# Reordering the start of a fused attention and token-mixing block on one core: loads, column sums, warm-up matmuls, early splits and the sums of phi(k)

## The chip, the cores and the metric

The kernel runs on one core of a Trainium2 chip. Its time is the device time of one execution in microseconds (us); the figure before the change is the median of three runs, and one more execution was taken with the hardware profiler. The engines are called as the profile calls them: PE is TensorE (PEld its weight loads), DVE is VectorE, ACT is ScalarE, POOL is GpSimd, SP is SyncE, which here only issues DMAs.

## The reference

`x` has S = 2048 tokens of D = 448 values. Two blocks follow each other, each with a modulated layer norm and a gated residual:

```python
mod = (silu(c) @ w_mod).reshape(1, 6, 1, 448)          # sa, ca, ga, sb, cb, gb
h = layernorm(x) * (1 + ca) + sa
x = x + ga * A(h)                                      # linear attention
h = layernorm(x) * (1 + cb) + sb
x = x + gb * B(h)                                      # token-mixing MLP

def A(x):                                              # 16 heads of 28
    q, k, v = split_heads(x @ wqkv)
    phi = lambda t: where(t > 0, t + 1, exp(t)) + 1e-6
    kv = einsum("hsd,hse->hde", phi(k), v); z = phi(k).sum(over s)
    return ((phi(q) @ kv) / (phi(q) . z + 1e-6)) @ wo

def B(x):                                              # F = 1792
    u = gelu(layernorm(x)^T @ w1 + b1)
    return (u @ w2 + b2)^T
```

Everything is fp32 in and out. The kernel splits an fp32 operand into a high and a low part (`hh` and `hl` for the token tiles, `wh` and `wl` for the weights, `pkh` and `pkl` for phi(k)) and sums the products of the parts on PE.

## The kernel before, in words

Tokens are cut into 16 tiles of 128 (`t`). The program is written out engine by engine in the order of the source (a manual schedule): each engine works through its own instructions in that order, and semaphores make it wait for the others' results. Buffers come from a pool of 74 slots that are used in turn, so a tile that is allocated waits until the last reader of the slot's former content is done. [...] DMAs are issued from SP's queue in the order of the source; those that add into their target (`accum_op`) are issued by POOL.

The stages follow each other: phase A computes q, k and phi(k) for all tiles and sums phi(k)^T x; then the small products with `wo`; then x is updated, normalised again and transposed; then the two big products with `w1` and `w2`. The change touches only the first part of phase A, roughly the first 90 us:

- `load_x(t)` fetches the tile x(t) for its statistics and `load_xt(t)` its transpose for the products; `load_first(j, ch)` fetches chunk `ch` of a transposed part of `w_mod` (`wt`), for j = 0 the shift and for j = 1 the scale.
- `spread` and `keep_warm(n)`: n matmuls of ones into a spare bank that keep PE busy until the first weights are there.
- `col_sum(j, ch)` multiplies a chunk with the spread silu(c) and sums it into one column of `col`. `row_part(1, ch)` adds the raw weights times a column of the shift to `accb`, one chunk after the other; `row_bias(1)` (L277) brings `accb` to PE, and `row_out(1)` makes the last rows of `wrow` of it, on ACT and then on DVE (L282).
- `projects(...)` and `close(t, 1)`: kp, the k part of tile t. It is accumulated from the parts without any layer norm and closed by one matmul with `wrow` and the rows of mean and root (L426).
- Those rows come from `a_stats_act` for tiles 0 and 1 (sums on ACT, two small steps and then the root as a power on POOL) and from `a_stats_dve` for the later pairs (statistics on DVE, `ve`, and the power on POOL, L339). `a_rows` writes them to `rowst` (L382, L385), `a_transpose` turns them on PE (`rw`, L391), and `a_copy` puts them into the last rows of `hl`.
- `a_split_high(t)` (ACT, L398) and `a_split_low(t)` (DVE, or POOL for tiles 0 and 2; L402) make `hh` and `hl`.
- `a_exp`, `a_pk` (DVE, L441) and `a_pk_parts` make phi(k), its high part and its low part. For tiles 3 to 12 the low part is finished by an adding DMA on POOL (L504); for tiles 2 to 12 a second adding DMA adds phi(k) into `pksum` (L508), which is read when the phase ends.
- `a_outer(t)` adds phi(k)^T x of a tile to `cacc`. The loop over t = 4 to 15 works four tiles behind on it (`KV_LAG`), and at t = 5, 7, 9 and 11 takes the statistics of the tiles t + 3 and t + 4.

Of the kernel before, what the change touches and what calls it, by code (L numbers as in the profile page):

```python
# [11 lines left out]
ALU = mybir.AluOpType  # L12
AX = mybir.AxisListType

P = 128
# [6 lines left out]
EPS = 1e-5  # L22
# [29 lines left out]
def block_kernel(ctx: ExitStack, tc: tile.TileContext, x, xt, wqkv, wo, w1, b1, w2, b2, c, wmod, wfirst, out):  # L52
# [69 lines left out]
    def load_x(t):  # L122
        X[t] = slot(f"x{t}")
        nc.sync.dma_start(X[t], xf[t * P:(t + 1) * P, :])
# [3 lines left out]
    def load_xt(t):  # L128
        XT[t] = slot(f"xt{t}", 512)
        nc.sync.dma_start(XT[t], xt[t])  # L130
# [8 lines left out]
    def load_first(j, ch, eng=nc.sync):  # L139
        wt[j, ch] = slot(f"wt{j}_{ch}", D + 1)  # L140
        eng.dma_start(wt[j, ch][:, :D], wfirst[j, ch])
        nc.gpsimd.memset(wt[j, ch][:, D:], 1.0 if j else 0.0)
# [12 lines left out]
    for ch in range(1, 4):  # L155
        load_first(1, ch)
        load_qkv(1, chs=(ch,))
        if ch == 1:
            load_xt(1)
    load_xt(2)  # L160
    for ch in range(4):
        load_first(0, ch)
    load_x(0)
    load_x(1)
    load_xt(3)
    load_xt(4)
    load_x(2)
# [14 lines left out]
    def keep_warm(n):  # L182
        for i in range(n):
            nc.tensor.matmul(warm[:, :P], ones, ones, start=True, stop=True)
# [30 lines left out]
    def col_sum(j, ch):  # L215
        if j not in col:
            col[j] = cst.tile([P, 4], F32, name=f"col{j}")
        p = slice(0, 64 if j == 0 and ch == 3 else P)
        w = wt.pop((j, ch))[p]
        nc.vector.scalar_tensor_tensor(w, w, 1.0, scr[p, :D + 1], op0=ALU.mult, op1=ALU.mult,  # L220
                                       accum_out=col[j][p, ch:ch + 1])
# [40 lines left out]
    def row_part(j, ch):  # L262
        if ch == 0:
            accb[j] = slot(f"accb{j}")
            nc.vector.tensor_scalar_mul(accb[j], raw_w[j, 0], col[0][:, 0:1])
        else:
            nc.vector.scalar_tensor_tensor(accb[j], raw_w[j, ch], col[0][:, ch:ch + 1], accb[j],
                                           op0=ALU.mult, op1=ALU.add)

    def row_sum(j):  # L270
        rowb[j] = bank(f"rowb{j}")
        ws = [Whi[j, ch] for ch in range(4)] + [Wlo[j, ch] for ch in range(3)]
        for i, w in enumerate(ws):
            nc.tensor.matmul(rowb[j][:ROWS, :D], sel_s, w, start=(i == 0), stop=False)
# [66 lines left out]
    def a_stats_act(ts):  # L341
        n = len(ts)
        g, ve = a_group(ts)
        sm = small.tile([P, n, 3], F32, name=f"as{ts[0]}", tag=f"as{n}")

        def one(i):
            t, s3 = ts[i], sm[:, i, :]
            nc.scalar.activation(junk, X[t], AF.Identity, accum_out=s3[:, 0:1])
            nc.scalar.activation(s3[:, 1:2], s3[:, 0:1], AF.Copy, scale=-1.0 / D)
            b_square(X[t], s3[:, 1:2], s3[:, 2:3], f"s{t}")  # L350

        def end():
            nc.gpsimd.tensor_scalar_mul(g[:, :, 0:1], sm[:, :, 0:1], 1.0 / D)
            nc.gpsimd.tensor_scalar(ve, sm[:, :, 2:3].to_broadcast([P, n, 2]), 1.0 / D, EPS,
                                    op0=ALU.mult, op1=ALU.add)
            a_pow(g, ve)
            groups[ts[0]] = g
        return one, end
# [37 lines left out]
    def a_split_high(t):  # L396
        heads[t] = (slot(f"hh{t}", 512, F32R), slot(f"hl{t}", 512, F32R))
        nc.scalar.activation(heads[t][0], XT[t], AF.Copy)  # L398

    def a_split_low(t):  # L400
        eng = nc.gpsimd if t in POOL_LOW else nc.vector
        eng.tensor_sub(heads[t][1], XT[t], heads[t][0].bitcast(F32))  # L402
        XT[t] = None

    def a_split(t):
        a_split_high(t)
        a_split_low(t)
# [88 lines left out]
    def a_pk_parts(t):  # L496
        pk = pkf.pop(t)
        hi, lo = moving(slot, f"pkh{t}"), moving(slot, f"pkl{t}")
        nc.scalar.activation(hi, pk, AF.Copy, bias=1e-6)
        if t in DVE_LOW:  # L500
            nc.vector.scalar_tensor_tensor(lo, pk, 1e-6, hi.bitcast(F32), op0=ALU.add, op1=ALU.subtract)
        else:
            nc.scalar.activation(lo, hi.bitcast(F32), AF.Copy, scale=-1.0, bias=1e-6)
            nc.gpsimd.dma_start(lo, pk, accum_op=ALU.add)  # L504
        if t < 2:
            pksum.append(pk)
        elif t in SUM_DMA:
            nc.gpsimd.dma_start(pksum[t % 2], pk, accum_op=ALU.add)  # L508
        else:
            nc.vector.tensor_add(pksum[1], pksum[1], pk)  # L510
        pks[t] = (hi, lo)


    cacc = []

# [13 lines left out]
                nc.tensor.matmul(cacc[ch][:, :D], xh[:, ch * P:(ch + 1) * P], kl, start=False, stop=False)  # L529

    spread()
    keep_warm(4)
    nc.scalar.activation(sel_s, sel_f, AF.Copy)
    col_sum(1, 0)
    a_split(0)
# [18 lines left out]
    def in_turn(t):  # L554
        return [(t, kind, ch) for ch in range(3) for kind in ("hh", "wl")] + [(t, "hh", 3)] + \
            [(t, "hl", ch) for ch in range(3)]
# [2 lines left out]
    w_row(1)  # L559
    act01, end01 = a_stats_act((0, 1))  # L560
    act01(0)
    for ch in range(4):
        col_sum(0, ch)
    row_sum(1)
    a_split_high(3)
    act01(1)
    end01()
    row_part(1, 0)
    a_split_low(3)
    for ch in (1, 2, 3):  # L570
        row_part(1, ch)
    a_split(4)
    projects(in_turn(3)[:4], 1, "kp")
    row_bias(1)
    projects(in_turn(3)[4:], 1, "kp")
    low = a_rows(0)
    first23, second23, end23 = a_stats_dve((2, 3))
    first23(0)
# [2 lines left out]
    second23(0)  # L581
    second23(1)
    end23()
    a_split_high(5)
    row_out(1)
    a_transpose(0)
    a_copy(0)
    a_copy(1)
# [7 lines left out]
    load_mod(2)  # L596
    load_xt(10)
    load_x(10)
    a_exp(0, kps[0])
    a_high(0)  # L600
    low = a_rows(2)
# [17 lines left out]
    a_pk(1, kps[1])  # L619
    low = a_rows(4)  # L620
    low()
    a_split(6)
    a_transpose(4)
    a_exp(2, kps[2])
    a_pk(2, kps[2])
# [15 lines left out]
    low = a_rows(6)  # L641
    a_pk_parts(2)
    low()
    a_split(7)
    wo_sb = []
    late = [t for t in range(NT) if t not in Q_EARLY.values()]
    for t in range(4, NT):
        if 5 < t < NT - 1:
            project(t + 1, 1, "kp")
        kp = close(t, 1) if t > 4 else kps[4]  # L650
        if t == 9:
            row_sum(0)
            row_bias(0)
        if t > 4:
            a_outer(t - KV_LAG)
        if t % 2 and 4 < t < NT - 2:
            a_transpose(t + 1)
        if t in Q_EARLY:
            a_q(Q_EARLY[t])
        if t == 12:  # L660
            mp = mod_sum2(2)
        pair = t % 2 and 7 < t + 3 < NT
        if pair:
            first, second, end = a_stats_dve((t + 3, t + 4))
            first(0)
        if 5 <= t < 9:
            w_low(0, t - 5)
        if pair:
            second(0)
        if 5 <= t < 9:  # L670
            row_part(0, t - 5)
        a_phi_q(t in Q_EARLY)
        if t == 9:
            a_exp(t, kp)
        if t % 2 and 4 < t < NT - 2:
            a_copy(t + 1)
            a_copy(t + 2)
        if t != 9:
            a_exp(t, kp)
        if 7 < t + 3 < NT:  # L680
            a_split_high(t + 3)
        a_pk_parts(t - 1)
        highs = HIGH_AT.get(t, (t - 2,))
        for i in highs[:1]:
            a_norm(i)
            a_high(i)
        if t % 2 == 0 and 4 < t < NT - 3:
            low = a_rows(t + 2)
        a_pk(t, kp)
        if t % 2 == 0 and 4 < t < NT - 3:  # L690
            low()
        if 7 < t + 3 < NT:
            a_split_low(t + 3)
        for i in highs[1:]:
            a_norm(i)
            a_high(i)
        if pair:
            first(1)
        for i in highs:
            a_low(i)  # L700
        if pair:
            second(1)
            end()
        if 4 <= t < 8:
            w_high(0, t - 4)
            if t == 7:
                w_row(0)
        if t == 9:
            row_out(0)
        if t == 12:  # L710
            mod_out(2, mp)
        if t in FETCH:
            load_xt(FETCH[t])
            load_x(FETCH[t])
        if 7 <= t < 11:
            mod_part(2, t - 7)
        if t == 11:
            mod_split(2)
        for j, i in MOD_AT.get(t, ()):
            mod_part(j, i)  # L720
        if t in (7, 10):
            load_mod(4 if t == 7 else 3)
        if t == 10:
            load_qkv(2, tslot)
        if t == 8:
            for g in range(4):
                w = tslot(f"wo{g}", parts=G)
                nc.sync.dma_start(w, wo[g * G:(g + 1) * G, :])
                wo_sb.append(w)
            b1c = cst.tile([P, NF], F32, name="b1c")  # L730
            nc.sync.dma_start(b1c, b1)
            b2c = cst.tile([P, NT], F32, name="b2c")
            nc.sync.dma_start(b2c, b2)
        if t >= 13:
            nc.vector.tensor_mul(wo_sb[t - 13], wo_sb[t - 13], mods[2][:G])
        load_to(PRE_LOAD.get(t, 0))
# [580 lines left out]
```

## Time and profile before

| | before |
|---|---|
| three runs, us | 437.96, 437.97, 438.0 |
| the profiled execution, us | 438.01 |
| its span, first to last instruction, us | 436.3 |
| granted PE clock over the span | 1.00 |
| PE busy | 429.2 us, 98%, 2337 matmuls |
| DVE busy | 360.6 us, 83% |
| ACT busy | 275.3 us, 63% |
| POOL busy | 117.9 us, 27% |
| DMA | 66.14 MB, 152 GB/s over the span |

A row of a timeline is: start in us, length in us, engine, line, operation, out<-in with their shapes, how many were put together (x), and in brackets the idle time of the engine before it and what ended it. "SPq" is an issue in SP's queue. A row of the waits is: who, for whom, us in all, times, longest. A row of the chain is: start, length, piece. A matmul of fp32 operands that are not split counts as two passes, and matmuls overlap, so the distance between two starts is their price.

### The profile page before, as it was taken

The numbers are of one execution on the slowest core, as the hardware profiler recorded it, in microseconds if no ns is written. First come the engines' busy times: TensorE is split into PE (matmuls) and PEld (weight loads), VectorE is DVE, ScalarE is ACT, GpSimd is POOL, SyncE is SP. The second block draws the span as 40 slices with busy tenths as digits, with TensorE's granted clock in tenths as the row PEclk, the third lists the DMA queues.
The fourth block names the chain that finished last, engine by engine and source line by source line (L and its number), as shares of the span: only waits on it lengthen the run. The fifth ranks groups of instructions, "written<-read, shape, count | busy, mean of one in ns | idle before, by whom it ended". The sixth has DMA issues, their size and how long they took to land.

```text
span 436.3 us, 7203 instructions
## 1 busy us (share of the span) xinstructions
PE 429.2 (98%) x2337; PEld 398.8 (91%) x2337; DVE 360.6 (83%) x809; ACT 275.3 (63%) x587; POOL 117.9 (27%) x200
## 2 busy tenths in 40 slices
PE   8899999999999999999999999999999999999996
PEld 8688899999899999999999999999999999999996
DVE  4899986689799999994679695829799988898894
ACT  5689867749657798886756263537464565645550
POOL 4335454100024477773300000010113131132010
PEclk9999999999999999999999999999999999999999
DMA  8997998465300036335417561587379977985430
GB/s 273 382 338 154 228 230 200 80 193 180 124 2 0 26 66 152 74 74 139 152 65 223 178 209 45 148 213 218 71 171 235 201 173 156 223 180 119 83 54 32
DMA packets 63941, 66.14 MB, mean 152 GB/s; under 512 B 4960, under 2 KB 55456, under 8 KB 63904
## 3 DMA queue, kind: packets, MB, share of 16 engines
q1 hardware_dynamic: 54832, 50.90, 37.6%
q0 software_dynamic: 8784, 14.32, 20.9%
q10 hardware_dynamic: 288, 0.46, 0.5%
q8 instruction: 18, 0.29, 0.3%
q14 instruction: 19, 0.16, 0.1%
HBM read 46.30 MB, written 7.34 MB: 123 GB/s over the span
## 4 chain that ended last, share of the span: by engine, by line
PE 89%; DVE 3%; DMA 2%; ACT 2%; POOL 1%; issue 1%; SPq 1%; DVEq 0%; ACTq 0%; POOLq 0%
PE y L1112 19%; PE up L897 10%; PE up L896 10%; PE up L895 10%; PE y L1113 9%; PE op L845 8%; PE qp L419 7%; PE cacc L525 6%; PE kp L419 3%; PE tq L820 1%; DMA wr<-in_qkv_dram 1%; DMA x<-in_A_x_dram 1%; PE qp L426 1%; PE kvb L776 1%; DVE st L367 1%
## 5 line engine op out<-in xcount | busy, mean ns | idle before, releaser
L896 PE MATMUL up<-h2l,ph 128*128 128x448 f32 x224 | 81.3, 363 | 0.0
L897 PE MATMUL up<-h2h,pl 128*128 128x448 f32 x224 | 81.2, 363 | 0.0
L895 PE MATMUL up<-h2h,ph 128*128 128x448 f32 x224 | 80.8, 361 | 0.0
L1067 POOL DMA_DIRECT2D a<-a x16 | 14.2, 959 | 138.0 <-DMA a<-in_B_w_dram 77.1
L896 PEld LDWEIGHTS up<-h2l,ph 128*128 128x128 f32 x224 | 42.0, 188 | 3.3 <-DVE h2l L892 0.3
L895 PEld LDWEIGHTS up<-h2h,ph 128*128 128x128 f32 x224 | 41.9, 187 | 3.0
L897 PEld LDWEIGHTS up<-h2h,pl 128*128 128x128 f32 x224 | 42.0, 188 | 2.5
L84 DVE TENSOR_TENSOR pl<-pr,ph 128x512 fp32r<-128x512 f32 x46 | 30.7, 685 | 4.2 <-ACT ph L83 3.3
L1118 ACT ACTIVATE cc<-y 128x448 f32<-128x448 f32 x24 | 13.0, 547 | 26.8 <-PE y L1113 26.8
L83 ACT ACTIVATE ph<-pr 128x512 fp32r<-128x512 f32 x46 | 27.6, 625 | 0.8 <-PE up L897 0.5
L1031 DVE TENSOR_TENSOR u<-u,mod 128x448 f32<-128x448 f32 x14 | 8.7, 621 | 21.6 <-ACT u L1030 21.4
L419 PE MATMUL kp<-wh,hh 128*128 128x448 f32 x64 | 24.4, 386 | 0.2 <-ACT rk L436 0.2
L845 PE MATMUL op<-wph,pth 128*128 128x448 f32 x64 | 24.5, 383 | 0.0
L1030 ACT ACTIVATE u<-up,b1c 128x448 f32<-128x448 f32 x14 | 8.8, 627 | 24.0 <-PE up L897 23.5
L1132 POOL DMA_DIRECT2D out_dram<-yt x14 | 12.7, 910 | 40.5 <-DVE yt L1123 31.1
L525 PE MATMUL cacc<-pkh,xh 128*128 128x448 f32 x64 | 23.6, 369 | 0.0
L419 PE MATMUL qp<-wh,hh 128*128 128x448 f32 x64 | 23.4, 366 | 0.0
L845 PE MATMUL op<-wpl,pth 128*128 128x448 f32 x64 | 23.1, 361 | 0.0
L802 POOL TENSOR_SCALAR den<-den 128x16 f32<-128x16 f32 x16 | 8.8, 549 | 43.6 <-DVE den L799 43.6
L525 PE MATMUL cacc<-pkl,xh 128*128 128x448 f32 x56 | 20.3, 362 | 0.0
L1073 DVE TENSOR_TENSOR a<-a,s 128x512 f32<-128x512 f32 (+1 forms) x32 | 18.5, 619 | 0.0
L1112 PE MATMUL y<-ub,a11h 128*128 128x448 f32 x56 | 18.2, 375 | 0.0
(233 smaller groups left out, 1362.3 us busy)
## 6 DMA issues: line engine op xcount, KB each, us to landing
pr<-in_B_w_dram SPq DMA_DIRECT2D x56, 256.0 KB, 3.0
a<-in_B_w_dram SPq DMA_DIRECT2D x32, 256.0 KB, 4.6
a<-in_B_w_dram SPq DMA_DIRECT2D x32, 192.0 KB, 4.6
xt<-in_xt_dram SPq DMA_DIRECT2D x16, 256.0 KB, 5.0
x<-in_A_x_dram SPq DMA_DIRECT2D x16, 224.0 KB, 5.0
wm<-in_B_wmod_dram SPq DMA_DIRECT2D x16, 196.0 KB, 4.9
out_dram<-x SPq DMA_DIRECT2D x14, 224.0 KB, 2.4
out_dram<-yt POOLq DMA_DIRECT2D x14, 224.0 KB, 5.5
```

The source lines that it names most:

```text
L83: nc.scalar.activation(hi, full, AF.Copy)
L84: nc.vector.tensor_sub(lo, full, hi.bitcast(F32))
L419: nc.tensor.matmul(pps[t, j][:, :D], a[:, ch * P:(ch + 1) * P], w, start=first, stop=False)
L525: nc.tensor.matmul(cacc[ch][:, :D], a[:, s], b, start=(t == 0 and i == 0), stop=(t == NT - 1 and i == len(todo) - 1))
L845: nc.tensor.matmul(opb[t][:, :D], a, b, start=(n == 0), stop=(n == len(todo) - 1))
L895: nc.tensor.matmul(ps[:, :D], hi[:, sl], mh, start=first, stop=False)
L896: nc.tensor.matmul(ps[:, :D], hi[:, sl], ml, start=False, stop=False)
L897: nc.tensor.matmul(ps[:, :D], lo[:, sl], mh, start=False, stop=last)
L1067: nc.gpsimd.dma_start(w, a, accum_op=ALU.add)
L1073: nc.vector.tensor_tensor(w, raw2[q, a][i], raw2[q, b][i], op=op)
L1112: nc.tensor.matmul(ps[:, :D], h[:, s], w, start=opens and r == 0, stop=False, skip_group_check=True)
L1113: nc.tensor.matmul(ps[:, :HD], l[:, s], wh, start=False, stop=closes and r == PAIRS - 1, skip_group_check=True)
```

## The change

It consists of seven edits, all in the order of the source except for three matmuls more and two small steps that change engine.

1. `load_x(0)` goes ahead of the four chunks of the shift, `load_x(1)` between the second and the third.
2. `keep_warm(7)` for `keep_warm(4)`.
3. The column sums of the shift are taken in pairs, each pair followed by its two `row_part`, and the statistics of tile 1 follow directly on those of tile 0; the split of tile 3 goes behind both.
4. The two small steps in `a_stats_act` ahead of the power go from POOL to DVE.
5. `a_split_high` of tiles 4 and 5 goes ahead of the statistics of tiles 2 and 3, the low part of tile 4 behind `row_out(1)`.
6. `a_split_high(6)` goes ahead of the first exponential.
7. The adding DMA into `pksum` is put on a list and issued by `sum_end()`, behind the pair's power on POOL.

```diff
     load_xt(2)
+    load_x(0)
     for ch in range(4):
+        if ch == 2:
+            load_x(1)
         load_first(0, ch)
-    load_x(0)
-    load_x(1)
     load_xt(3)
...
         def end():
-            nc.gpsimd.tensor_scalar_mul(g[:, :, 0:1], sm[:, :, 0:1], 1.0 / D)
-            nc.gpsimd.tensor_scalar(ve, sm[:, :, 2:3].to_broadcast([P, n, 2]), 1.0 / D, EPS,
+            nc.vector.tensor_scalar_mul(g[:, :, 0:1], sm[:, :, 0:1], 1.0 / D)
+            nc.vector.tensor_scalar(ve, sm[:, :, 2:3].to_broadcast([P, n, 2]), 1.0 / D, EPS,
                                     op0=ALU.mult, op1=ALU.add)
             a_pow(g, ve)
...
         elif t in SUM_DMA:
-            nc.gpsimd.dma_start(pksum[t % 2], pk, accum_op=ALU.add)
+            late_sum.append((pksum[t % 2], pk))
...
+    late_sum = []
+
+    def sum_end():
+        while late_sum:
+            nc.gpsimd.dma_start(*late_sum.pop(0), accum_op=ALU.add)
...
     spread()
-    keep_warm(4)
+    keep_warm(7)
...
     act01(0)
-    for ch in range(4):
+    for ch in (0, 2):
         col_sum(0, ch)
+        col_sum(0, ch + 1)
+        row_part(1, ch)
+        row_part(1, ch + 1)
     row_sum(1)
-    a_split_high(3)
     act01(1)
     end01()
-    row_part(1, 0)
-    a_split_low(3)
-    for ch in (1, 2, 3):
-        row_part(1, ch)
-    a_split(4)
+    a_split(3)
     projects(in_turn(3)[:4], 1, "kp")
     row_bias(1)
     projects(in_turn(3)[4:], 1, "kp")
+    a_split_high(4)
+    a_split_high(5)
     low = a_rows(0)
...
     end23()
-    a_split_high(5)
     row_out(1)
+    a_split_low(4)
     a_transpose(0)
...
+    a_split_high(6)
     a_exp(0, kps[0])
...
-    a_split(6)
+    a_split_low(6)
     a_transpose(4)
...
     low()
+    sum_end()
     a_split(7)
...
         if pair:
             second(1)
             end()
+        sum_end()
```

Three places show what moves. The first is SP's queue of loads, from the transpose of tile 2 on (`xt` the transposes, `wt` the shift's chunks, `x` the tiles for the statistics). Before:

```order
L130 DMA xt_136<-in_xt_dram 128x512
L141 DMA wt_0_138<-in_first_dram 128x448
L141 DMA wt_1_141<-in_first_dram 128x448
L141 DMA wt_2_144<-in_first_dram 128x448
L141 DMA wt_3_147<-in_first_dram 128x448
L124 DMA x_150<-in_A_x_dram 128x448
L124 DMA x_152<-in_A_x_dram 128x448
```

Now:

```order
L130 DMA xt_136<-in_xt_dram 128x512
L124 DMA x_138<-in_A_x_dram 128x448
L141 DMA wt_0_140<-in_first_dram 128x448
L141 DMA wt_1_143<-in_first_dram 128x448
L124 DMA x_146<-in_A_x_dram 128x448
L141 DMA wt_2_148<-in_first_dram 128x448
L141 DMA wt_3_151<-in_first_dram 128x448
```

The two tiles x stand one place behind xt and three places further on; the chunks of wt are one and two places later, and nothing behind them has moved.

The second is DVE's work between the last low part of the weights (`wh_3`) and the first phi(k); `wt` are the column sums, `accb` the running row, `hl` the low parts of tiles 3, 4 and 5, `mv` and `ve` mean and variance, `wrow` the closing rows. Before:

```order
L220 SCALAR_TENSOR_TENSOR wt_0_138,col_202<-wt_0_138,scr 128x449
L220 SCALAR_TENSOR_TENSOR wt_1_141,col_202<-wt_1_141,scr 128x449
L220 SCALAR_TENSOR_TENSOR wt_2_144,col_202<-wt_2_144,scr 128x449
L220 SCALAR_TENSOR_TENSOR wt_3_147,col_202<-wt_3_147,scr 64x449
L265 TENSOR_SCALAR accb_309<-wr_0_117,col_202 128x448
L402 TENSOR_TENSOR hl_301<-xt_154,hh_300 128x512
L267 SCALAR_TENSOR_TENSOR accb_309<-wr_1_122,col_202,accb_309 128x448
L267 SCALAR_TENSOR_TENSOR accb_309<-wr_2_129,col_202,accb_309 128x448
L267 SCALAR_TENSOR_TENSOR accb_309<-wr_3_134,col_202,accb_309 128x448
L402 TENSOR_TENSOR hl_316<-xt_156,hh_315 128x512
L382 CAST rowst_104<-mv_282 128x4x2
L367 BN_STATS st_334<-x_158 128x6
```

Now:

```order
L221 SCALAR_TENSOR_TENSOR wt_0_140,col_202<-wt_0_140,scr 128x449
L221 SCALAR_TENSOR_TENSOR wt_1_143,col_202<-wt_1_143,scr 128x449
L266 TENSOR_SCALAR accb_293<-wr_0_117,col_202 128x448
L268 SCALAR_TENSOR_TENSOR accb_293<-wr_1_122,col_202,accb_293 128x448
L221 SCALAR_TENSOR_TENSOR wt_2_148,col_202<-wt_2_148,scr 128x449
L221 SCALAR_TENSOR_TENSOR wt_3_151,col_202<-wt_3_151,scr 64x449
L268 SCALAR_TENSOR_TENSOR accb_293<-wr_2_129,col_202,accb_293 128x448
L268 SCALAR_TENSOR_TENSOR accb_293<-wr_3_134,col_202,accb_293 128x448
L354 TENSOR_SCALAR mv_285<-as_287 128x2
L355 TENSOR_SCALAR ve_286<-as_287 128x4
L403 TENSOR_TENSOR hl_315<-xt_154,hh_314 128x512
L383 CAST rowst_104<-mv_285 128x4x2
```

The sums `wt` and `accb` are interleaved, the low part of tile 3 stands behind `accb`, and the two small steps `mv` and `ve` have come in ahead of `rowst`. The low part of tile 4, ahead of `rowst` before, now follows `wrow` further down.

The third is POOL's queue from the low part of phi(k) of tile 4 on; `pkl<-pk` finishes a low part, `pk<-pk` adds into `pksum`, `mv<-ve,roots` is the power of a pair of tiles. Before:

```order
L504 DMA pkl_573<-pk_530 128x448
L508 DMA pk_393<-pk_530 128x448
L339 TENSOR_TENSOR mv_554<-ve_555,roots 128x2x2
L504 DMA pkl_633<-pk_583 128x448
L508 DMA pk_449<-pk_583 128x448
L504 DMA pkl_695<-pk_644 128x448
L508 DMA pk_393<-pk_644 128x448
L339 TENSOR_TENSOR mv_677<-ve_678,roots 128x2x2
```

Now:

```order
L505 DMA pkl_576<-pk_532 128x448
L340 TENSOR_TENSOR mv_557<-ve_558,roots 128x2x2
L519 DMA pk_399<-pk_532 128x448
L505 DMA pkl_636<-pk_585 128x448
L519 DMA pk_455<-pk_585 128x448
L505 DMA pkl_698<-pk_646 128x448
L340 TENSOR_TENSOR mv_680<-ve_681,roots 128x2x2
L519 DMA pk_399<-pk_646 128x448
```

At each pair the power now stands ahead of the sum that was issued just before it; the low parts keep their places. In the slots' turn this also changes who takes which buffer: the slot that the phi(k) tile of token tile 6 leaves was taken by phi(k) of tile 9 before, and is taken by the low part of tile 12 now, one place later in DVE's work.

## The prediction

> **What bounds the kernel now.** I read the page first, then the table of waits of TensorE alone, then the chain of waits over the first 24 us, then the timelines of the five engines around each wait, and last the landings of single DMAs.
>
> ```profile
> span 436.3 us, 7203 instructions
> PE 429.2 (98%) x2337; PEld 398.8 (91%) x2337; DVE 360.6 (83%) x809; ACT 275.3 (63%) x587; POOL 117.9 (27%) x200
> PE rowb L277 <- DVE accb L267: 1.6, 1, 1.6
> PE warm L184 <- DVE roots L105: 1.1, 1, 1.1
> PE kp L426 <- DVE wrow L282: 0.5, 1, 0.5
> PE kp L419 <- ACT rk L436: 0.2, 1, 0.2
> PE rw L391 <- DVE rowst L385: 0.2, 1, 0.2
> ```
>
> TensorE is busy for 98% of the span. The five lower rows are all of its listed waits in the whole run, 3.6 us, and all lie before 44 us. So a change to the first 60 us can win only what it takes from these waits, and keeps it to the end unless another wait opens. The 1.1 us before the first matmul are untouched, so 2.5 us are to be had at most. The chain shows what stands behind the waits of 1.6 and 0.5 us (start, length, piece):
>
> ```profile
> 9.02 4.84 DMA x<-in_A_x_dram
> 13.88 0.68 ACT junk L348 x2
> ...
> 17.79 0.43 POOL ve L354
> ...
> 18.29 1.50 POOL mv L339
> ...
> 19.82 0.17 DVE rowst L382
> ...
> 21.58 0.64 DVE wrow L282
> ...
> 22.35 0.46 PE kp L426
> ```
>
> The x tile of token tile 0 is issued at 9.02 and lands at 13.86. ScalarE then takes the statistics of tiles 0 and 1, GpSimd their roots, VectorE writes them to rowst, and behind that stand wrow and the closing matmul at 22.35. Beside it runs a second path on VectorE, the sums accb, for which the L277 matmul waits.
>
> **The change part by part.** The sum is made against the profiled run's own 438.01 us: its span of 436.3 us and 1.7 us around it. The median of the three timed runs is 437.97, 0.04 less, so no correction is needed.
>
> *Loads, and the sums in pairs.*
>
> ```profile
> 6.56 2.18 SPq L141 DMA_DIRECT2D wt<-in_first_dram  x4
> 11.48 0.66 ACT L251 ACTIVATE wrow<-wr,col 64x448 fp32r<-64x448 f32 x1
> 12.29 0.62 DVE L220 SCALAR_TENSOR_TENSOR wt<-wt,scr 128x449 f32<-128x449 f32 x1
> 14.46 0.44 DVE L265 TENSOR_SCALAR accb<-wr,col 128x448 f32<-128x448 f32 x1
> 16.76 2.12 DVE L267 SCALAR_TENSOR_TENSOR accb<-wr,col,accb 128x448 f32<-128x448 f32 x3
> 18.79 0.69 DVE L402 TENSOR_TENSOR hl<-xt,hh 128x512 fp32r<-128x512 f32 x1
> ```
>
> The four chunks of wt were issued from 6.56 on and x(0) at 9.02, so one place of SyncE's queue is (9.02 - 6.56) / 4 = 0.62 us. With 4.84 us to landing, x(0) now lands at 6.56 + 4.84 = 11.40, x(1) three places later at 13.25, and the last two chunks two places later than before, at 13.86 and 14.48. The same six transfers fill the same six places, so later loads are not moved.
>
> ScalarE is free at about 12.1 (11.48 + 0.66). The statistics of two tiles with a split between them took from 13.88 to 17.79, 3.9 us; without the split they end before 16.0. VectorE's column sums take (14.46 - 12.29) / 4 = 0.54 us each. In pairs: two sums to 13.38; the first accb step 0.44, to 13.82; the second 2.12 / 3 = 0.71, to 14.53; two sums to 15.6 (the last starts at 15.07, 0.6 us after its chunk has landed); two more steps, 1.42, to 17.0. Before, accb was done at 16.76 + 2.12 = 18.88. The low part of tile 3 is no longer in its midst, nor any wait for ScalarE.
>
> The two small steps that leave GpSimd (L353, L354) now stand on VectorE behind accb: two such small steps, by rowst's 0.17 us each, 0.3 us, to 17.3. Their upper bound is GpSimd's 0.43 for the second. The roots can then start at about 17.35 where they started at 18.29. They took 1.50 us, so end at 18.85 where they ended at 19.79: **0.95 us earlier**. That shift goes through rowst, the two statistics steps and wrow to the close at 22.35. Its bounds are 0.8 and, with roots as short as a later one shown below (1.17 us), 1.3.
>
> [...]
>
> *Three more warm-up matmuls.*
>
> ```profile
> 6.33 2.08 PE L184 MATMUL warm<-ones 128*128 128x128 f32 x8
> 8.06 0.72 PE L419 MATMUL kp<-wh,hh 128*128 128x448 f32 x1
> ...
> 9.70 0.40 PE L419 MATMUL kp<-wh,hl 128*128 128x448 f32 x1
> ...
> 14.94 0.97 PE L274 MATMUL rowb<-wh,sel_s 128*98 128x448 f32 x4
> ...
> 18.93 0.99 PE L277 MATMUL rowb<-accb,sel_b 128*98 128x448 f32 x2 [1.62 <-DVE accb L267]
> ```
>
> Four warm-up matmuls run as eight passes from 6.33 to 8.06, 0.217 us each; three more are 1.30 us, and kp starts at 9.36. Of the 30 kp matmuls of tiles 0 to 2, the first four took 8.06 to 9.70, 0.41 each, the other 26 took (14.94 - 9.70) / 26 = 0.20: TensorE's clock doubled near 9.7 (the page's clock row shows full speed in every slice; only the matmuls show the step). If it does so at the same time, one matmul is slow and 29 are not: 9.36 + 0.41 + 29 x 0.20 = 15.6, 0.67 later than 14.94. TensorE stood ready for L277 at 18.93 - 1.62 = 17.31, so now at 17.98. accb is there at 17.0, so the wait of 1.62 is gone and L277 starts **0.95 us earlier**. What is late next is wrow: TensorE reached the close at 22.35 - 0.49 = 21.86, now 20.9, and wrow allows 21.4. Both paths move by the same 0.95 us and half a microsecond of waiting stays.
>
> *Early high parts.* The high part of tile 6 leaves ScalarE's stretch behind the first exponentials for its idle time ahead of them, and tiles 4 and 5 go ahead of row_out, where ScalarE waits for L277 anyhow. This removes most of the 0.2 us for which TensorE waits for rk in the table: **0.15 us**. The low part of tile 4 moves on VectorE from ahead of the roots' arrival to behind wrow: 0.69 us in a full stretch, of which 0.46 us are idle now:
>
> ```profile
> 24.09 0.62 DVE L441 SCALAR_TENSOR_TENSOR pk<-ek,rk 128x448 f32<-128x448 f32 x1 [0.46 <-ACT rk L436]
> ```
>
> The rest, 0.2 us, makes VectorE later at the low part of tile 8, of which TensorE takes it over: **0.1 us lost**, 0.2 without any cover left.
>
> *Sums behind the roots.* The accumulating DMA into pksum now stands behind the roots in GpSimd's queue.
>
> ```profile
> 40.05 1.24 POOL L508 DMA_DIRECT2D pk<-pk  x1
> 40.73 1.97 POOL L339 TENSOR_TENSOR mv<-ve,roots 128x4 f32<-128x4 f32 x1
> 42.73 0.17 DVE L382 CAST rowst<-mv 128x8 fp32r<-128x8 f32 x1 [0.48 <-POOL mv L339]
> 43.56 0.32 PE L391 MATMUL rw<-ident,rowst 128*98 128x128 f32 x1 [0.17 <-DVE rowst L385]
> 49.57 1.17 POOL L339 TENSOR_TENSOR mv<-ve,roots 128x4 f32<-128x4 f32 x1
> ```
>
> The roots at 40.73 took 1.97 us because the DMA's issue held GpSimd to 41.29; those at 49.57 took 1.17. That is 0.8 us on GpSimd, more than TensorE's wait for rowst at 43.56. The listed 0.17 us goes, and with the start that overlaps the matmul before it up to 0.35: **0.3 us**. Behind the roots now stand the sum and the next tile's pkl; GpSimd had 2.7 us of idle time ahead of such a pkl (row at 47.66 below), so it isn't late. The sums themselves are needed at the end of the stage, 40 us later, but they hold buffers; that is the second rival.
>
> The sum: 0.95 + 0.15 - 0.1 + 0.3 = 1.3 us, and with the lower ends 0.8 + 0.1 - 0.2 + 0.17 = 0.9, with the upper ones 1.3 + 0.2 + 0.35 = 1.85. I take 1.4, a little above the sum, since VectorE's wait of 0.48 us for these roots at 42.73 also goes and covers the 0.1: 438.0 - 1.4 = **436.6 us**, within 436.1 and 437.1.
>
> **The rivals.** *First, the clock doubles later.* Before, a late doubling was hidden by the 1.62 us at L277; now only the 0.5 us ahead of the close hide it. Each microsecond of delay costs half of one (0.41 against 0.20 a matmul). It came 3.4 us after the warm-up resumed at 6.33, which speaks for a fixed distance and so for 9.7 again. If it may come anywhere in a further 3.4 us, the loss is up to 1.7 - 0.5 = 1.2 us: 436.7 to 437.9. [...] Chance 0.13.
>
> *Second, the later sums hold a buffer.*
>
> ```profile
> 47.66 0.88 POOL L504 DMA_DIRECT2D pkl<-pk  x1 [2.66 <-ACT pkl L503]
> DMA to landing us min/median/max: 7.8/7.8/7.8
> 48.21 1.23 POOL L508 DMA_DIRECT2D pk<-pk  x1
> DMA to landing us min/median/max: 8.6/8.6/8.6
> 55.80 0.86 POOL L508 DMA_DIRECT2D pk<-pk  x1 [2.98 <-DVE xn L479]
> DMA to landing us min/median/max: 4.5/4.5/4.5
> 56.90 0.62 DVE L441 SCALAR_TENSOR_TENSOR pk<-ek,rk 128x448 f32<-128x448 f32 x1 [1.57 <-ACT pkh L499]
> 59.59 0.63 DVE L282 TENSOR_TENSOR wrow<-rowb,wrow 2x448 fp32r<-2x448 f32 x1
> 61.42 0.37 PE L426 MATMUL qp<-wrow,hl 98*128 98x448 f32 x1
> ```
>
> Each landing row belongs to the DMA above it. The sum of tile 6, issued at 48.21, landed at 56.8, and VectorE went on at 56.90: the ScalarE step that the row names was long done, so it was this landing that freed a buffer. From there VectorE's queue ran 3.3 us to the end of wrow at 60.22, 1.2 us ahead of TensorE at 61.42. Now this sum goes behind the roots (1.17 us) and the tile that takes its buffer stands one step of about 0.55 us later in the queue, so 2.75 us remain to wrow's end. TensorE, 1.4 us earlier, wants wrow at 60.0: any landing up to 57.2 is free. If the DMA takes 8.6 us from its own issue (48.21 - 1.4 + 2.6, about 49.4), it lands at 58.0 and 0.8 us are lost: 437.4. Against it: pkl ahead of it in the same queue landed at 55.5, 1.3 us before it, so it was the queue that took the time, and a later issue behind the same transfer costs nothing. Chance 0.15.
>
> *Third, slower.* The same place, if the queue is served so that the sum lands no sooner than the next one did, 55.80 + 4.5 = 60.3: wrow would be done at 63.05, 1.6 us after TensorE wanted it before the change: 439.6. It decides from a landing at 58.7 on (58.7 + 2.75 = 61.4); over 0.2% is lost from 59.6. Chance 0.07.
>
> *Fourth, the change does little of what it says*: wt's chunks, now later, hold the column sums. They have 0.6 us; a microsecond more in landing costs 0.4 us of accb, and TensorE's new slack of 1 us at L277 covers that, not the roots: 437.0 to 437.4. Chance 0.05.
>
> **How the numbers follow.** The forecast has 0.60, and the rivals 0.13, 0.15, 0.07 and 0.05. About 0.2%, 0.88 us, is what a measurement of this kernel can tell from no change: faster means under 437.1. That is the forecast (0.60), a third of the clock's case (0.05) and some of the second and fourth (0.04): 0.69. Slower is the third: 0.07. The rest, 0.24, is within. The range reaches from 436.0, the upper ends' 1.85 us and 0.1 for the timing, to 437.9, the clock's and the second rival's far ends.
>
> **What would show it.** Right: x lands near 11.4 and ScalarE's first L349 starts at 12.1; TensorE waits nowhere at L278; the close of tile 0 at 21.4 with half a microsecond for wrow; rw of tile 8 at 42.2 without a wait; the same 1.4 us at every later matmul. Wrong: kp steps of 0.4 us beyond 9.8; VectorE waiting past 57.2 and TensorE for wrow near 60; any TensorE wait after 44 us; or a shift at 44 us that is given back later.

## The result and the profile after

The changed kernel takes **436.34 us** (median of six runs, 436.10 to 436.52), the kernel before 437.99 in runs beside it (437.96 to 438.39). The ratio is 0.9960 with a 95% interval of 0.9948 to 0.9973: 1.65 us faster. The profiled execution is the shortest of the six, 436.1 us with a span of 434.4, 1.9 us under the span before.

The head of the page, then all waits of TensorE:

```profile
span 434.4 us, 7215 instructions
PE 428.8 (99%) x2343; PEld 397.3 (91%) x2343; DVE 360.4 (83%) x811; ACT 274.9 (63%) x587; POOL 116.0 (27%) x198
```

```profile
PE warm L185 <- DVE roots L105: 1.1, 1, 1.1
PE kp L427 <- DVE wrow L283: 0.8, 1, 0.8
PE rw L392 <- DVE rowst L386: 0.2, 1, 0.2
```

The wait of 1.62 us for `accb`, the one for `rk` and the one for `rowst` at 43.56 are gone. The wait for `wrow` at the close grew from 0.5 to 0.8 us, and a small one for `rowst` of tiles 0 and 1 is new. Now the timeline of TensorE (start, length, piece), with the places of the prediction:

```profile
6.10 1.83 PE L185 MATMUL warm<-ones 128*128 128x128 f32 x14
7.68 0.45 PE L420 MATMUL kp<-wh,hh 128*128 128x448 f32 x1
...
16.74 0.95 PE L278 MATMUL rowb<-accb,sel_b 128*98 128x448 f32 x2
...
20.85 0.64 PE L427 MATMUL kp<-wrow,hl 98*128 98x448 f32 x2 [0.76 <-DVE wrow L283]
...
27.67 0.47 PE L420 MATMUL kp<-wh,hh 128*128 128x448 f32 x1
...
30.42 0.47 PE L532 MATMUL cacc<-pkh,xl 128*128 128x448 f32 x1
...
34.67 0.47 PE L427 MATMUL kp<-wrow,hl 98*128 98x448 f32 x1
...
37.65 0.47 PE L420 MATMUL kp<-wh,hl 128*128 128x448 f32 x1
...
41.57 0.37 PE L532 MATMUL cacc<-pkl,xh 128*128 128x448 f32 x1
41.78 0.27 PE L392 MATMUL rw<-ident,rowst 128*98 128x128 f32 x1
...
430.68 0.27 PE L1123 MATMUL y<-ut,a22l 128*128 128x224 f32 x1
```

Of before, beside the rows in the prediction:

```profile
29.47 0.47 PE L419 MATMUL kp<-wh,hh 128*128 128x448 f32 x1 [0.19 <-ACT rk L436]
...
43.02 0.37 PE L525 MATMUL cacc<-pkl,xh 128*128 128x448 f32 x1
...
432.55 0.27 PE L1113 MATMUL y<-ut,a22l 128*128 128x224 f32 x1
```

| place | before | after | gained so far |
|---|---|---|---|
| close of tile 0 | 22.35 | 20.85 | 1.50 |
| first kp of tile 6 | 29.47 | 27.67 | 1.80 |
| last cacc ahead of rw of tile 8 | 43.02 | 41.57 | 1.45 |
| rw of tile 8 | 43.56 | 41.78 | 1.78 |
| last matmul | 432.55 | 430.68 | 1.87 |

So the close is 1.50 us earlier with the loads, the sums in pairs and the roots, and 0.3 more are gained where the early high parts take the wait for `rk` away. Some 0.35 are given back between 30 and 42 us, where VectorE has no listed idle time and TensorE's steps at 30.42, 34.67 and 37.65 last 0.47 us where such steps last 0.36: VectorE's `xl`, which the step at 30.42 reads, moved with the close (31.27 to 29.81, 1.46 us) and not with TensorE's 1.80. The last 0.33 come from the roots of tile 8. Hardly anything changes afterwards. That `xl` before:

```profile
31.27 0.55 DVE L489 TENSOR_TENSOR xl<-xn,xh 128x384 fp32r<-128x384 f32 x1
```

The other engines at these places now:

```profile
11.74 0.56 ACT L349 ACTIVATE junk<-x 128x448 f32<-128x448 f32 x1
16.56 0.16 DVE L354 TENSOR_SCALAR mv<-as 128x2 f32<-128x2 f32 x1
16.63 0.16 DVE L355 TENSOR_SCALAR ve<-as 128x4 f32<-128x4 f32 x1
16.87 1.41 POOL L340 TENSOR_TENSOR mv<-ve,roots 128x4 f32<-128x4 f32 x1 [3.75 <-DVE ve L355]
18.32 0.17 DVE L383 CAST rowst<-mv 128x8 fp32r<-128x8 f32 x1 [0.93 <-POOL mv L340]
...
29.81 0.56 DVE L490 TENSOR_TENSOR xl<-xn,xh 128x384 fp32r<-128x384 f32 x1
...
39.25 1.56 POOL L340 TENSOR_TENSOR mv<-ve,roots 128x4 f32<-128x4 f32 x1 [0.32 <-DVE ve L374]
40.62 0.90 POOL L519 DMA_DIRECT2D pk<-pk  x1
...
48.82 1.07 POOL L519 DMA_DIRECT2D pk<-pk  x1
DMA to landing us min/median/max: 5.5/5.5/5.5
```

The roots of tiles 0 and 1 end at 18.28 in place of 19.79. Those of tile 8 last 1.56 us in place of 1.97; no DMA issue stands directly ahead of them now. The sum of tile 6, issued at 48.82, lands at 54.3.

### The profile page after: what moved, and what is told of

It reads as the page before. It is cut to its first block, busy times and chain, and to the rows that moved or that the text cites. A ratio compares the mean times of both kernels' runs of the same rounds, so it can differ in the third digit from the quotient of the medians.

```text
span 434.4 us, 7215 instructions
## 1 busy us (share of the span) xinstructions
PE 428.8 (99%) x2343; PEld 397.3 (91%) x2343; DVE 360.4 (83%) x811; ACT 274.9 (63%) x587; POOL 116.0 (27%) x198
## 4 chain that ended last, share of the span: by engine, by line
PE 94%; DMA 2%; DVE 2%; POOL 0%; issue 0%; ACT 0%; SPq 0%; DVEq 0%
PE y L1122 19%; PE up L905 10%; PE up L906 10%; PE up L907 10%; PE y L1123 9%; PE op L855 8%; PE cacc L532 8%; PE qp L420 7%; PE kp L420 5%; PE tq L830 1%; DMA wr<-in_qkv_dram 1%; DMA xt<-in_xt_dram 1%; PE kp L427 1%; PE qp L427 1%; PE kvb L786 1%; PE wp L922 1%
```

## The experiments

The second column is the median, the third has the single runs (.43 stands for the same full microsecond as the number ahead of it). The kernel before ran beside each: 437.93 us (12 runs) beside the first four, 438.07 (17) beside the next four, 438.05 (17) beside the last four.

| kernel | us | runs | ratio, 95% |
|---|---|---|---|
| again | 436.46 | 436.23, .43, .46, .67, .68 | 0.9954 to 0.9979 |
| loads_only | 436.74 | 436.47, .53, .62, .74, .74, .75, 437.20 | 0.9961 to 0.9982 |
| warm4 | 436.58 | 436.06, .31, .42, .74, .82, 437.01 | 0.9957 to 0.9981 |
| high_old | 436.35 | 436.20, .27, .35, .49, .67 | 0.9952 to 0.9977 |
| sums_in_place | 436.75 | 436.54, .75, .75, .81, 437.05 | 0.9957 to 0.9981 |
| end_pool | 436.05 | 435.49, .80, 436.05, .46, .50 | 0.9940 to 0.9964 |
| roots_early | 435.85 | 435.24, .31, .47, 436.24, .29, .47 | 0.9937 to 0.9962 |
| before_warm7 | 438.10 | 437.74 to 438.34 (11) | 0.9991 to 1.0008 |
| early_warm4 | 435.56 | 435.21, .50, .56, .59, .70 | 0.9930 to 0.9955 |
| early_warm10 | 436.16 | 435.18, .37, .60, 436.71, .93, 437.14 | 0.9943 to 0.9971 |
| early_warm0 | 436.03 | 435.86, .93, 436.03, 437.06, .16 | 0.9951 to 0.9975 |
| sum_later | 437.30 | 437.17 to 437.54 (11) | 0.9975 to 0.9992 |

The intervals are some 0.5 us to either side, so differences of a few tenths between neighbours are read from the profiles.

**again.** The changed kernel without an edit.

> The changed kernel as it stands, for a second profiled execution of it. Theory A, the doubling of TensorE's clock is not tied to the kernel's own work: it came before 6 us in the first profile (436.1 us, the shortest of six) and near 9.7 in the profile of before; here it may come anywhere from 5.8 to 9.8, the first warm-up passes and kp matmuls taking 0.2 and 0.4 us before it, and the time goes with it: 436.1 with an early step, 436.3 to 436.5 with a late one. Theory B, the changed kernel's own start brings the step forward: the profile shows it before 6 us again, and the times still spread over 436.1 to 436.5 for another reason.

Its timeline of TensorE at the start:

```profile
1.11 2.93 PE L185 MATMUL warm<-ones 128*128 128x128 f32 x12 [1.11 <-DVE roots L105]
3.86 1.55 PE L208 MATMUL scr<-ident,sc 112*128 112x112 f32 x8
5.34 0.38 PE L210 MATMUL scr<-ones 1*128 1x1 f32 x2
5.64 1.83 PE L185 MATMUL warm<-ones 128*128 128x128 f32 x14
```

The eight passes of `scr` start at 3.86 here and before. Before, they ended only at 5.82 (0.245 us a pass); here the next row starts at 5.34. At full speed they need half the time (a warm-up pass takes 0.113 us here, 0.217 before), so the clock doubled near 4.9 us; in the first profile near 5.8. The step moves from run to run, as theory A says, but two early steps in one kernel fit B too; the next runs decide.

**Part by part.** The first part alone, on the kernel before:

```
 load_xt(2)
+load_x(0)            # then wt 0, 1, x(1), wt 2, 3
-for ch in range(4): col_sum(0, ch)
+for ch in (0, 2): col_sum(0, ch); col_sum(0, ch + 1); row_part(1, ch); row_part(1, ch + 1)
 ... act01(1); end01() with its two small steps on nc.vector; a_split(3); a_split(4)
```

> The kernel before, with the first part of the change alone: x ahead of wt's chunks, column sums and accb steps in pairs, the low part of tile 3 behind them, and the two small steps ahead of the roots on VectorE. Theory A: this part carries most of the gain, 1.1 to 1.3 us (the close of tile 0 moved 1.5 us in the profile of the changed kernel, 0.3 of which was there at 6 us already): 436.7 to 436.9. Rival, the prediction's own term: 0.95, 437.05. Rival 2, without the other parts VectorE is late behind the close and gives half of it back by 44 us: 437.4.

436.74, 1.19 us under before, with an interval of 0.8 to 1.7.

```profile
20.93 0.64 PE L427 MATMUL kp<-wrow,hl 98*128 98x448 f32 x2 [0.76 <-DVE wrow L283]
```

In its profile the close of tile 0 stands at 20.93, 1.42 earlier than before, and the wait of 0.2 us for `rk` and the delay of 0.3 at `rw` of tile 8 are still there. This part carries three quarters of the gain. By its time alone the price of 0.95 in the prediction is possible too; by the close it was too low.

The three others take one part out of the changed kernel.

```
-keep_warm(7)
+keep_warm(4)
```

> The changed kernel with four warm-up matmuls at this place, as before the change, in place of seven. Theory A: TensorE only stands longer at the close of tile 0 (0.76 us of waiting become 1.1 to 1.4), since wrow sets it: 436.2 to 436.5, no difference. Rival 1, the warm-ups hold the clock up: the first kp matmuls take 0.4 us each for longer, and 436.6 to 436.9. Rival 2, the warm-ups stand on the path after all: 435.7 to 436.0.

```
-a_split_high(4); a_split_high(5)     # ahead of row_out
-a_split_high(6)                      # ahead of the first exponentials
+a_split(4), a_split_high(5) and a_split(6) where they stood before
```

> The changed kernel with the high parts of tiles 4 to 6 (and the low part of tile 4) at their old places. Theory A: TensorE's wait of 0.2 us for rk ahead of the kp of tile 6 comes back and costs 0.2 to 0.37, and of the three or four delays of 0.1 us that VectorE's fuller queue made between 30 and 43 us (kp<-wh,hl, kp<-wrow, cacc<-pkh,xl of 0.47 us in place of 0.36) most go: 436.3 to 436.5, hardly a difference. Rival, the prediction's sum: 0.15 won less 0.1, so 436.4 with no trace of the delays. Rival 2: the early parts are worth their whole 0.37: 436.7.

```
-late_sum.append((pksum[t % 2], pk))
+nc.gpsimd.dma_start(pksum[t % 2], pk, accum_op=ALU.add)
```

> The changed kernel with each sum of phi(k) issued where it stood before, ahead of the roots. Theory A: the roots near 39 us are held by the DMA's issue again (about 1.9 us in place of 1.56), VectorE waits 0.3 to 0.5 us for them, TensorE 0.2 to 0.35 for rowst at the transpose of tile 8: 436.6 to 436.7. Rival: VectorE is behind anyhow between 30 and 42 us, so the roots are not what it waits for: 436.3 to 436.4. Third, the later sums hold a buffer (the prediction's second rival): undone here, 435.9 to 436.2.

warm4 is not faster and its interval overlaps again's nearly whole. Its profile (an early step, near 4.7) shows where three warm-ups fewer went: TensorE waits 0.40 us for `wh` at 7.14 and 0.33 for `wl` at 9.67, and at the close it waits 0.77 for `wrow` as before, not the expected 1.1 to 1.4. So with an early clock the warm-ups fill waits for the weights and are off the path. Three of its six runs are at 436.7 to 437.0, above what was expected; its profiled run is not one of them, and why is open.

high_old cannot be told from again by its time. Its timeline shows both halves of the trade:

```profile
28.05 0.48 PE L420 MATMUL kp<-wh,hh 128*128 128x448 f32 x1 [0.19 <-ACT rk L437]
29.89 0.55 DVE L490 TENSOR_TENSOR xl<-xn,xh 128x384 fp32r<-128x384 f32 x1
```

The wait for `rk` is back: rw of tile 6 to this kp is 0.45 us (27.60 to 28.05), where the changed kernel has 0.10. In return the delays at 30.42 and 34.67 are gone, and from the close on it reaches 42 us at the same distance as again to 0.05 us. VectorE's `xl` stands 8.92 us behind the close here (20.97) and before, and 8.96 in the changed kernel: the early high parts bring TensorE forward, but not VectorE, for which it then waits. So edits 5 and 6 are worth nothing that these times can tell.

By the medians sums_in_place is 0.3 to 0.4 above the changed kernel; measured against the kernel before beside each, 0.15 to 0.33. That is less than the times can tell, but its timelines of GpSimd and TensorE show the size:

```profile
39.41 1.96 POOL L340 TENSOR_TENSOR mv<-ve,roots 128x4 f32<-128x4 f32 x1
41.72 0.37 PE L532 MATMUL cacc<-pkl,xh 128*128 128x448 f32 x1
42.24 0.32 PE L392 MATMUL rw<-ident,rowst 128*98 128x128 f32 x1
```

The roots last 1.96 us again, and TensorE's `rw` starts 0.52 us after the matmul ahead of it in place of 0.21: 0.3 us, the prediction's term.

**before_warm7.** The kernel before with `keep_warm(7)`.

> The kernel before, with seven warm-up matmuls in place of four and nothing else. Theory A: the 1.62 us for which TensorE waits for accb there hide them: 437.9 to 438.05, no difference, and the profile says when the clock doubles in a kernel whose first 6 us are those of before. Rival, the warm-ups bring the doubling forward: a step before 9 us, at the same time in all.

```profile
9.58 0.61 PE L419 MATMUL kp<-wh,hh 128*128 128x448 f32 x1
10.03 0.36 PE L419 MATMUL kp<-wh,hl 128*128 128x448 f32 x1
...
18.82 0.99 PE L277 MATMUL rowb<-accb,sel_b 128*98 128x448 f32 x2 [0.61 <-DVE accb L267]
```

No difference: the wait for `accb` is 0.61 us where it was 1.62, and takes the 1.0 us up. The clock doubled near 9.8 in the profiled run, so the three more warm-ups did not bring the step forward there.

**The small steps.** They went to VectorE to be short, but stand there behind `accb`. ScalarE's statistics end near 15.2. end_pool puts them back on `nc.gpsimd`; roots_early leaves them on VectorE, ahead of the last two accb steps:

```
+act01(1)
 for ch in (0, 2):
     col_sum(0, ch); col_sum(0, ch + 1)
+    if ch: end01()
     row_part(1, ch); row_part(1, ch + 1)
 row_sum(1)
-act01(1); end01()
```

> The changed kernel with the two small steps ahead of the roots of tiles 0 and 1 on GpSimd again. There they need not stand behind accb on VectorE (16.56 us), but take 0.23 and 0.43 us and start when ScalarE's statistics end, at 15.2. Theory A: the roots then start at about 15.9 in place of 16.87, and the close is 0.5 to 0.8 us earlier, until TensorE itself sets it: 435.6 to 435.9, so the move to VectorE was a loss. Rival, the prediction's working: the move was right, and with the steps on GpSimd the roots start later: 436.4 to 436.7.

> The changed kernel with the two small steps on VectorE put ahead of the last two accb steps (15.25 to 16.64 us) and not behind them. ScalarE's statistics end near 15.2, so the roots start at about 15.5 in place of 16.87; accb is done 0.15 us later, which TensorE meets with a small wait at most. Theory A: the close is set by the roots' chain, and moves by the 0.76 us for which TensorE waits there, then TensorE itself sets it: 435.5 to 435.8. Rival 1: VectorE, which had no idle time from 20 to 44 us, sets the pace behind the close, and 0.3 us at most stay: 436.0 to 436.2. Rival 2: roots beside the accb steps take longer than 1.41 us, 436.3.

The roots and TensorE in end_pool:

```profile
16.34 1.49 POOL L340 TENSOR_TENSOR mv<-ve,roots 128x4 f32<-128x4 f32 x1
6.33 3.36 PE L185 MATMUL warm<-ones 128*128 128x128 f32 x14
9.34 0.72 PE L420 MATMUL kp<-wh,hh 128*128 128x448 f32 x1
10.60 0.40 PE L420 MATMUL kp<-wh,hh 128*128 128x448 f32 x1
20.94 0.73 PE L427 MATMUL kp<-wrow,hl 98*128 98x448 f32 x2
```

and in roots_early:

```profile
15.71 1.41 POOL L340 TENSOR_TENSOR mv<-ve,roots 128x4 f32<-128x4 f32 x1 [2.43 <-DVE ve L355]
19.98 0.65 PE L427 MATMUL kp<-wrow,hl 98*128 98x448 f32 x2
```

The roots start 0.5 and 1.2 us earlier than 16.87 (in end_pool not the expected 1.0: the second small step starts at 15.52 and takes 0.74 us, where 0.43 was expected). end_pool has one run and roots_early three at 435.2 to 435.5; the fastest of the changed kernel's eleven is 436.10. But the profiled run of end_pool met a late step, near 10.7: 14 warm-up passes of 0.217 us, kp from 9.34, and TensorE at the close at 20.94 without a listed wait, though `wrow` was there at 20.41 (19.78 + 0.63). There TensorE itself sets the close. In roots_early the runs fall into two groups about a microsecond apart, and the profiled one, of the lower group, had its step near 4.1. There theory A holds; that the upper group is the late clock, as in end_pool, is what the next runs ask.

**Fewer and more warm-ups where they count.** roots_early with 4, 10 and 0 of them:

```
-keep_warm(7)
+keep_warm(4)     # or 10, or 0
```

> The kernel with the two small steps ahead of the last accb steps (roots_early), with four warm-up matmuls in place of seven. There the times fell into two groups, 435.2 to 435.5 and 436.2 to 436.5. Theory A, the groups are the phase of TensorE's clock: with an early doubling VectorE and TensorE meet at the close of tile 0 at 19.98 us, with a late one (near 10 us) TensorE gets there near 20.9 whatever the roots do. Three warm-ups fewer are six slow passes, of which 0.65 us remain at the close in the late case: the upper group goes to 435.6 to 435.8, the lower stays at 435.3, and nothing is above 436.0. Rival: the groups have another cause (loads, the state of the chip), and the upper one stays at 436.2 to 436.5.

> As roots_early with ten warm-up matmuls. Theory A: with a late doubling all passes are slow and TensorE reaches the close 0.65 us later still, 436.9 to 437.1; with an early one six more passes are 0.66 us, of which the wait of 0.4 us for wl near 9.6 takes most, 435.3 to 435.8. So the groups move apart. Rival, the warm-ups call the early doubling: no late group, all at 435.3 to 435.8.

> As roots_early with no warm-up matmul at this place (those ahead of the sigmoid's spreading stay). TensorE then waits for wh from about 5.5 to 7.2 us. Theory A, the doubling is not tied to this stretch: 435.2 to 435.7 as with four. Rival: a gap of over a microsecond keeps the clock down, the doubling comes after 10.6, the latest seen so far, and the time is 436.3 or more in most runs.

With 4, 7 and 10 warm-ups the upper group is at 435.50 to 435.70, 436.24 to 436.47 and 436.71 to 437.14: some 0.7 us for each three, as the worked price of 0.65. The lower group stays at 435.2 to 435.6. The profiled run of early_warm4 (435.50, counted to its upper group) shows a late step (kp 0.37 us apart up to 9.70, 0.20 from 10.02 on) and its close 0.92 before end_pool's:

```profile
20.02 0.65 PE L427 MATMUL kp<-wrow,hl 98*128 98x448 f32 x2
```

So the time at which the clock doubles explains the groups, in place and in size. It is not shown in every link: no run of the upper group of roots_early or early_warm10 has a profile, and in early_warm4 the two groups are too close to be told apart by time. early_warm4 is the fastest kernel here, 435.56, with a ratio of 0.9930 to 0.9955. From the changed kernel's 0.9948 to 0.9973 the intervals do not quite part it, but its slowest run (435.70) is faster than the fastest of the changed kernel's eleven (436.10).

early_warm0 fits neither theory wholly. Its timeline:

```profile
7.46 0.47 PE L420 MATMUL kp<-wh,hh 128*128 128x448 f32 x1 [1.49 <-ACT wh L248]
8.48 0.38 PE L420 MATMUL kp<-wh,hh 128*128 128x448 f32 x1
8.69 0.55 PE L420 MATMUL kp<-wh,hl 128*128 128x448 f32 x1
...
12.02 0.62 PE L420 MATMUL kp<-wl,hh 128*128 128x448 f32 x2
12.48 0.76 PE L420 MATMUL kp<-wh,hl 128*128 128x448 f32 x3
```

The clock had doubled near 5.4, but after the gap of 1.49 us it fell back at 8.7 and doubled again near 12.1. So warm-ups do something: they close a gap, which the fall followed in this profile; after the gaps of 0.40 and 0.33 us in warm4 none came. The granted clock of the three runs at 435.9 to 436.0 is 0.996, that of the two at 437.1 is 1.000. So such a fall is not what made those two slow. They have no profile, so the rival's later first doubling can neither be shown nor excluded, and their cause is open.

**sum_later.** Each sum of phi(k) one more tile later:

```
-while late_sum:
+while len(late_sum) > keep:     # 1, from tile 14 on 0
```

> The changed kernel with each sum of phi(k) issued one more tile later: that of tile 6 at about 51.9 us in place of 48.8, those of tiles 5 and 7 some 6 us later than now. Theory A, the sum holds a buffer that the low part of the tile six later takes (the prediction's second and third rival): with landings 5.3 us after the issue, VectorE stands 2.6 us and more for that of tile 12 (54.56 us now), the wrow of the q projection is 0.9 us and more too late, and the tiles beside it cost as much or more: 437.2 to 446. Rival: what held VectorE at 56.9 us before was not this buffer, and the time stays at 436.2 to 436.6 with no wait of VectorE over 0.6 us between 50 and 65 us.

VectorE's timeline, and TensorE's at the end of the stage:

```profile
54.84 0.62 DVE L442 SCALAR_TENSOR_TENSOR pk<-ek,rk 128x448 f32<-128x448 f32 x1 [1.20 <-ACT hh L399]
86.65 0.62 DVE L511 TENSOR_TENSOR pk<-pk,pk 128x448 f32<-128x448 f32 x1 [1.21 <-DMA pk<-pk]
104.48 1.73 PE L786 MATMUL kvb<-cs,wr 128*112 128x112 f32 x15 [0.63 <-DVE cs L777]
```

In this kernel phi(k) of tile 9 takes the slot of tile 5's, whose sum was issued at 49.01 and took 5.7 us: it landed at 54.7, and VectorE went on at 54.84. (The row names ScalarE's `hh`, which ended at the same time; this step doesn't read it, and what it reads, `ek` and `rk`, was done at 51.65.) So a sum does hold a slot, as far as these times show. But those 1.20 us cost nothing there: `wrow` is done at 58.15 (57.52 + 0.63), and TensorE uses it at 59.73. The loss of 0.9 us is elsewhere: the last sums land late, VectorE waits 1.21 us for one at 86.65 and reaches `cs` 1.2 us later than in the changed kernel, and TensorE waits there. The time is at the low end of what was expected, the place is another: the low part of tile 12, for which a wait of 2.6 us was expected, starts at 55.38 right behind phi(k).

## Why the prediction was right, point by point

- **Loads and sums in pairs: right in mechanism, too low in size.** 0.95 us was forecast, within 0.8 to 1.3; the close moved by 1.50 in the profile, and loads_only is worth 1.19. ScalarE started at 11.74 where 12.1 was forecast, since the whole start was 0.2 to 0.3 us earlier: `scr` ended sooner under the early clock, and VectorE was at the first of these column sums at 11.99 in place of 12.29. These 0.30 us are the luck of the clock in these two profiles and not the change's, which leaves it 1.2 of the 1.50; loads_only, 0.23 earlier at that sum, leaves 1.19 of 1.42. The other 0.25 above the forecast are small pieces: the two steps took 0.23 us and not 0.3 (16.56 to 16.79), the roots 1.41 and not 1.50, `accb` was done at 16.6 (16.9 in end_pool, under a late clock) and not 17.0.
- **Warm-ups: right that they are hidden, wrong on the clock.** kp from 9.36 and TensorE at the close at 20.9 are what end_pool measured, 9.34 and 20.94. In the other profiles with seven warm-ups, before_warm7 apart, the step came early, kp started at 6.8 to 7.7, and TensorE had more time to spare. Half a microsecond of waiting was to remain at the close; 0.76 did.
- **Early high parts: the net right to 0.1, the mechanism of the loss wrong.** +0.15 less 0.1 was forecast; +0.30 and -0.35 were measured (1.50 to 1.80 to 1.45 in the table). The loss was put down to the low part of tile 4 in VectorE's queue. That part cost hardly anything: VectorE's idle 0.46 us at 24.09 covered it, and `xl` came only 0.04 later behind the close. The gain was given back because VectorE, without idle time up to 42 us, set the pace from 30 us on, and nothing had made it earlier.
- **Sums behind the roots: right.** 0.3 forecast, 0.33 in the profile, 0.3 when undone (0.52 for 0.21 us at `rw`). That VectorE's wait of 0.48 at 42.73 goes did not cover the loss of the high parts, as the 1.4 had supposed: that loss comes ahead of it.
- **The sum.** 1.3 was worked out and 1.4 taken; 1.65 was measured, 1.47 in the repeat, 1.9 in the profiled run. The term that was mis-sized is that of the first part, by 0.25 us without the early start and 0.55 with it. The forecast took edits 2 and 4 for parts of the gain or free; end_pool and early_warm4 show that a better order and fewer warm-ups were left, worth up to 0.8 us.
- **First rival, the clock: its mechanism is there, its loss is not.** The step does move from run to run. No fixed distance shows: from the warm-up's resuming at 6.33 it was 3.4 us in the kernel before and 4.4 in end_pool. The 1.2 us were worked out from a step up to 3.4 us later than 9.7, which was an estimate that no run shows: the latest step came near 10.7. The half microsecond ahead of the close covers the latest step seen to within 0.1 us (20.94 against 20.85). Both profiles of the changed kernel itself had an early one, so a late step in it was not seen. It costs about a microsecond only where the roots no longer hide it, in roots_early, if the upper group there is the late clock.
- **Second and third rival, the sum of tile 6.** It landed at 54.3, ahead of the 57.2 up to which a landing was free: 5.5 us after its issue at 48.82, where 8.6 us, or a landing at 60.3, had been feared. VectorE's wait at 56.9 is gone. That a late landing does hold VectorE, and that slack at `wrow` takes it up, sum_later shows.
- **Fourth rival.** VectorE's third column sum started at 14.16 without a wait; the chunks were in time.

## What to carry to other kernels

When a change takes away the wait that lay behind a varying stretch, list the single runs: two groups say that a hidden variation now sets the end, and a median between them describes no run (in roots_early 435.24 to 435.47 and 436.24 to 436.47, median 435.85). A step that moves to a faster engine is priced by when it ends in that engine's queue, not by its length: here the two steps were 0.4 us shorter on VectorE (0.23 us for both, against 0.23 and 0.42 on GpSimd in the kernel before) and the roots behind them 0.5 us later than with the steps on GpSimd (16.87, against 16.34 in end_pool). In a stretch where a second engine has no idle time, an early piece for the first moves a wait rather than removing it: here 0.30 us were won at 27.67 and 0.35 given back by 41.57.

## What the runs showed of the hardware

In these runs the doubling of TensorE's clock did not follow the kernel. In fourteen profiles of these kernels, in which the first matmul starts near 1.11, it came between 4.1 and 5.8 us in ten and between 9.7 and 10.7 in four, and never between. loads_only, whose first 6 us are those of the kernel before (9.7), doubled near 5.6; end_pool, with the first 14 us of the changed kernel (5.8 and 4.9), near 10.7. In early_warm0, after a gap of 1.49 us, it fell back, and was away for 3.4 us (8.7 to 12.1), in which a kp matmul took 0.37 us and not 0.20; the granted clock of that run was 0.996, while the clock row of its page, in slices of 10.9 us, shows 9 tenths or more throughout. The early steps come 3.0 to 4.7 us after the first matmul, the late ones 8.6 to 9.6 us after it; what sets either, no run here explains.
